# The first expert of a mixture-of-experts kernel: where its weight splitting, its last gate and its counts are issued

## The chip, the cores and the metric

The kernel runs on one core of a Trainium2 chip. The metric is the time of one execution in device microseconds, the median of several runs. The engines are named as the profile names them: PE (TensorE; PEld is its weight loading), DVE (VectorE), ACT (ScalarE), POOL (GpSimd), and SP (SyncE), which issues most of the DMAs. A "q" behind a name (PEldq, ACTq) is that engine's own sequencer.

## The reference, cut to what matters

```
def reference(...):                      # all in float32
    o = attention(q_l, k_l, v_l, q_g, k_g, v_g)      # 4 batches, 8 heads, 512 local + 32 global rows, 64 wide
    x = o as [2304, 512]                             # one token per row
    # mixture of 8 experts, one expert per token
    logits = x @ w_gate;  e_idx = argmax(logits)
    gate_w = softmax(logits)[e_idx];  eom = sigmoid(x @ w_output_gate)
    out[mask_e] = gate_w * eom[:, e] * (relu(x[mask_e] @ w1[e]) @ w2[e])      # w1 512x1024, w2 1024x512
    # a last layer
    h = out @ w_in;  g = P(h) / Q(h);  return g @ w_out
```

The routing depends on the data: how many tokens each expert has, and which, is known on the chip only when the gate of the last of four batches has run.

## The kernel before, in words

**Order of the program.** The order of the instructions is written out by hand. Python generators stand for streams of work, and a loop around the matrix products takes a step of such a stream at fixed places. Each engine executes its own instructions in the order in which the program issues them, so an instruction that waits holds up everything behind it on its engine.

**Precision.** Every factor is split into a high part (a cast on ACT, L696 for weights) and a low part (the difference, L700), and each product is three matmuls. `split_piece` makes one of 16 pieces (128x512) of an expert's weights; its mode says who makes the low part: "act" means DVE, "act_pool" means POOL. `split_set` goes through the pieces, and after every second one it issues the load of the next raw weights on SP's queue (L686), into the buffer that the two pieces have left.

**The first expert.** `wide(0, ...)` computes it for 296 tokens, taken from the first three batches, while the gate of the last batch still runs. It has 8 steps of a first product (L903, 12 matmuls) and 8 of a second (L915, 12 matmuls), the second two steps behind. After every six matmuls it takes one step of the stream `woven`. I call such a place a hook; there are 32.

- `woven` before: in hooks 1 to 16 two steps of the last gate (GS = 2), and from hook 9 on one piece of the first half of expert 1's weights, its low parts on POOL and DVE in turn. At hook 17 all that is left of the gate is issued at once, and with hook 17 the list PLAN0 begins: s is a piece of the second half (hooks 18 to 25), g a gather of token rows (two at hook 17), x a scaling of a gathered block on ACT (hooks 23, 24, 26, 27), p its transposition and splitting (`prep`, hooks 24, 25, 28, 30). `lists` (the list of tokens, transposed on PE at L650) runs at hooks 17 to 20.
- The gate's last batch: transposes on PE (L519), some small DVE instructions, the counting matmuls (L554), then five pairs of one-hot rows on DVE (L605, L609) that five matmuls (L620) turn into the table of tokens. From it come the row indices for the gathers (`places`). `counts` then makes the counts and offsets of the experts in 19 small DVE instructions (L747 to L767).
- After the 32 hooks `end` copies the result from PSUM (L921) and stores it. Then every engine loads the counts into registers, in two loads (L1058, L1060), and two branches follow: `single` for the third block of 128 tokens of expert 0 (L1064; it is taken in this run, L870 to L886), and a loop for the rest (L1066; skipped). Then the blocks 2 and 3 of expert 1 are scaled on ACT (L797), transposed on PE (L810) and split, and expert 1 begins (L903 with the tile xa).

The transposes of `prep` go through one PSUM tile (pt) as long as the first expert runs: the next block is transposed only when ACT (L790) and DVE (L791) have read the one before.

The weights of expert 0 itself are split during the attention before it (SM0 is the mode), the last pieces at its very end.

Of the kernel before, what the change touches and what calls it, by code (L numbers as in the profile page):

```python
# [11 lines left out]
I32 = mybir.dt.int32  # L12
# [7 lines left out]
B, H, SL, SG, D = 4, 8, 512, 32, 64  # L20
S = SL + SG
NT = B * S
NP = H // 2
DM = H * D
E = 8
F1 = 1024
NBLK = NT // 128
NCOL = E * NBLK


WN = 15
SLAST, GW, GS, SPL, AH = 1, 3, 2, 8, (0, 0, 14, 1, 2, 0, 2, 24, 2)
NW = 0
XR = lambda nc: nc.scalar.copy
XG = lambda nc, h: nc.vector.tensor_copy
# [6 lines left out]
BASE, MOST, FIRST, LAG = 256, 512, 296, 2  # L42
# [4 lines left out]
def plan(n, **at):  # L47

    o = [""] * n
    for t in "scxpg":  # L50
        for k in at.get(t, ()):
            o[k] += t
    return o
# [8 lines left out]
R7 = 4  # L62
L9 = {-1: (0, 1, 2, 3)}
XLO = lambda nc, i: (nc.vector, nc.gpsimd)[i % 2]
PLAN0 = plan(16, s=range(1, 9), g=(0, 0, 1, 2, 11, 12, 14, 15), x=(6, 7, 9, 10), p=(7, 8, 11, 13))
TR = (1, 1), (2, 2)
YC = 256
EL, EW = 0, 11
# [19 lines left out]
CH = (4, 3, 4, 3, 3)  # L88
ER = {"ab": 1, "q": 2, "u": 2, "r0": 1}
CQ = lambda nc: nc.sync  # L90
SM0 = "act_pool"
MASK = (0, 1, 2, 3, 1, 2, 3, 4)
KT, KV, KX = 4, 5, 7
KG, LL = 3, 2
# [9 lines left out]
class Build:  # L104
# [391 lines left out]
    def gate(self, b, xT=None, woven=0):  # L496
# [107 lines left out]
        for i in range(nb):  # L604
# [6 lines left out]
            for _ in range(2 + (OY if b < B - 2 else 0)):  # L611
                if i:
                    next(tail, None)
                yield
        for _ in wait():
            yield
        for _ in tail:
            yield
# [6 lines left out]
        if last:  # L625
            self.places(self.idx[:, 0:NCOL], self.tab)
            nc.gpsimd.memset(self.idx[:, NCOL:], NT)
            self.counts()
        elif b == B - 2:
            self.places(self.idx0, self.tab[:, 0:3])  # L630
            nc.vector.tensor_copy(self.cnt0, self.run_cnt[0:1, 0:1])
# [113 lines left out]
    def counts(self):  # L745
        nc, c = self.nc, self.cnt_f
        nc.vector.memset(c, 0.0)  # L747
        nc.vector.tensor_tensor(out=self.cnt_i[:, 0], in0=self.run_cnt[0:1, :], in1=self.small[0:1, 8:16], op=ALU.subtract)
        nc.vector.tensor_copy(c[:, 0, 1:8], self.cnt_i[:, 0, 0:7])
        for n, k in enumerate((1, 2, 4)):  # L750
            o = c[:, n + 1] if n < 2 else self.cnt_i[:, 1]
            nc.vector.tensor_copy(o[:, 0:k], c[:, n, 0:k])
            nc.vector.tensor_tensor(out=o[:, k:8], in0=c[:, n, k:8], in1=c[:, n, 0:8 - k], op=ALU.add)

        k, n0, o = self.cnt0, self.cnt_i[:, 0, 0:1], self.cnt_x
# [3 lines left out]
        nc.vector.scalar_tensor_tensor(out=o[:, 3:4], in0=n0, scalar=FIRST + 128, in1=o[:, 3:4], op0=ALU.is_gt, op1=ALU.max)  # L759
        nc.vector.tensor_scalar(out=o[:, 2:3], in0=n0, scalar1=127, scalar2=None, op0=ALU.add)  # L760
        nc.vector.tensor_scalar(out=o[:, 2:3], in0=o[:, 2:3], scalar1=7, scalar2=None, op0=ALU.logical_shift_right)
        nc.vector.tensor_tensor(out=o[:, 2:3], in0=o[:, 2:3], in1=o[:, 3:4], op=ALU.mult)

        f = o[:, 4:5]
        nc.vector.tensor_reduce(out=f, in_=self.cnt_i[:, 0], axis=AX.X, op=ALU.max)
        nc.vector.tensor_scalar(out=f, in0=f, scalar1=MOST, scalar2=None, op0=ALU.is_gt)
        nc.vector.scalar_tensor_tensor(out=f, in0=self.cnt_i[:, 1, E - 1:E], scalar=128 * CH[0], in1=f, op0=ALU.is_lt, op1=ALU.max)  # L767


    def expert_tiles(self, pool):  # L770
# [7 lines left out]
        self.cnt_i = cp.tile([1, 2, E], I32, name="cnt_i")  # L778
        self.cnt_f = cp.tile([1, 4, E], F32, name="cnt_f")
        c = cp.tile([1, 6], I32, name="cnt_x")  # L780
        self.cnt0, self.cnt_x = c[:, 0:1], c[:, 1:6]

    def gather(self, j, ix, n=NT, rows=128):

# [30 lines left out]
    def experts(self, st, first, gate):  # L815
# [114 lines left out]
                pass  # L930
            return end

        def todo(e, plan, half=None, blocks=(), gathers=()):


            sp = self.split_set(e + 1, SPLIT_MODE if e < E - 1 else MODE7, half)
            if e == E - 1:
                self.rest = sp
            k = NCONV * (e - 1)
            gs, xs, ps = iter(gathers), iter(blocks), iter(blocks)  # L940
            for do in plan:
                for c in do:
                    if c == "s":
                        next(sp, None)
                    elif c == "c":
                        self.conv_step(k)
                        k += 1
                    elif c == "g":
                        for eb in islice(gs, 1):
                            self.gather(eb[1], col(*eb))  # L950
# [79 lines left out]

        def woven():

            g, sp = self.gate(B - 1, woven=GW), todo(0, "s" * 8, 0)
            for n in count():
                for _ in range(GS):
                    next(g, None)
                if n >= SPL:
                    next(sp, None)
                yield
                if n >= WN:  # L1040
                    break
            for _ in g:
                pass
            for _ in sp:
                pass

            yield from weave(todo(0, PLAN0, 1, blocks(1, (0, 1)) + blocks(0, (2, 3)),
                                  blocks(1, (0, 1)) + blocks(0, (2, 3)) + blocks(2, (0, 1)) + blocks(1, (2, 3))),
                             self.lists())


        acc = [ps_a.tile([128, 512], F32, tag=f"acc{m}", name=f"acc{m}") for m in range(4)]
        wide(0, 0, FIRST, self.xs, woven(), False, acc)()
        gate.close()
        pools.append(PP("ps_t2", 1))
        self.conv_init(P("cv"))
        self.f32.append(spare)
        vals = nc.values_load_multi_w_load_instructions(self.cnt_i.rearrange("a b e -> a (b e)"), min_val=0, max_val=NT)[1]  # L1058
        cnt, off[:] = vals[:E], vals[E:]
        x = nc.values_load_multi_w_load_instructions(self.cnt_x, min_val=0, max_val=NBLK)[1]  # L1060
        more0, j0, end0, again0, rare = x
# [347 lines left out]
```

## Time and profile before

| | us |
|---|---|
| median of 3 runs (lowest, highest) | 834.62 (830.66, 835.91) |
| the profiled execution | 836.12 |
| its span in the trace | 834.6 |
| first expert: first L903 to first matmul of the third block (L870) | 152.98 to 194.89 |
| third block: to the first L903 of expert 1 | 194.89 to 214.02 |

PE is busy for 787.6 us of the span (94%), DVE 605.9, ACT 543.7, POOL 374.2. The mean granted clock of PE is 0.979 of full speed.

Two views are used most. The view by windows gives, for each stretch, the busy time of each engine and the clock that PE was granted (1.00 is 2.4 GHz, 0.50 is 1.2 GHz). The timeline merges equal instructions that follow each other into one row: start, duration, engine, line, operation, tiles and count, and in brackets how long the engine had been idle before and what it then waited for. The rows themselves stand below.

### The profile page before, as it was taken

Reading aid. Unit: us, or ns where it says so; the run is one execution under the profiler, and the core shown is the slowest. Engines: PE = TensorE matmul, PEld = TensorE weight load, DVE = VectorE, ACT = ScalarE, POOL = GpSimd, SP = SyncE. Lnnn points to the kernel's source line nnn. Section 1 sums busy time; section 2 is a strip of 40 time slices with the busy share of each in tenths; the row PEclk is TensorE's granted clock in tenths of the full one; section 3 lists DMA queues with packets and bytes.
Section 4 is the critical chain, followed back from the end, with each engine's and each line's share of the span. In section 5 each row is a group of like instructions: output and inputs, shape, how many; then the busy total and the mean of one; then the engine's idle time right before and its main releaser. Section 6 shows DMA issues by size and latency. Waiting matters only on the chain. (4 is left out here: it accounts for less than half of the span.)

```text
span 834.6 us, 17062 instructions
## 1 busy us (share of the span) xinstructions
PE 787.6 (94%) x6093; PEld 669.2 (80%) x6094; DVE 605.9 (73%) x1436; ACT 543.7 (65%) x1221; POOL 374.2 (45%) x422
## 2 busy tenths in 40 slices
PE   7999998969899999999998999999999999999995
PEld 4776766767898999998885788899878888988983
DVE  3769778681556777874377999778878885888784
ACT  3667776542645666663447888768777775788774
POOL 2445555561434665652253787532243234222432
PEclk7999999979899999999999999999999999999998
DMA  8899993464373988986263432010010001000100
GB/s 298 267 281 302 289 304 83 131 195 136 127 253 127 308 302 282 323 292 206 81 187 103 126 93 60 13 51 26 13 38 25 2 1 51 0 1 1 39 1 38
DMA packets 50957, 113.90 MB, mean 136 GB/s; under 512 B 8963, under 2 KB 22548, under 8 KB 48810
## 3 DMA queue, kind: packets, MB, share of 16 engines
q1 hardware_dynamic: 42202, 98.23, 36.6%
q0 software_dynamic: 4288, 10.06, 3.7%
q10 hardware_dynamic: 4368, 4.34, 1.5%
q8 instruction: 55, 0.90, 0.5%
q14 instruction: 44, 0.36, 0.1%
HBM read 96.99 MB, written 19.56 MB: 140 GB/s over the span
## 5 line engine op out<-in xcount | busy, mean ns | idle before, releaser
L1190 POOL TENSOR_TENSOR q<-q,ab 128x384 f32<-128x384 f32 (+1 forms) x80 | 101.8, 1273 | 203.2 <-ACT q L1189 195.0
L1226 PE MATMUL acc<-slot,gh 128*128 128x512 f32 x544 | 171.1, 395 | 3.8 <-ACT gh L1198 2.0
L700 POOL TENSOR_TENSOR slot<-raw,slot 128x512 fp32r<-128x512 f32 x80 | 111.1, 1393 | 78.9 <-ACT slot L696 74.4
L1119 PE MATMUL ph<-x2c,slot 128*128 128x512 f32 (+1 forms) x576 | 132.5, 379 | 5.7 <-DVE u L1192 3.9
L1119 PEld LDWEIGHTS ph<-x2c,slot 128*128 128x128 f32 x576 | 106.5, 189 | 26.3 <-DVE u L1192 5.1
L1226 PEld LDWEIGHTS acc<-slot,gh 128*128 128x128 f32 x544 | 101.1, 187 | 25.9 <-ACT gh L1198 2.9
L1226 PE MATMUL acc<-slot,gl 128*128 128x512 f32 x272 | 107.6, 396 | 0.2 <-DVE gl L1199 0.2
L915 PE MATMUL acc<-hT,slot 128*128 128x256 f32 (+1 forms) x768 | 105.2, 288 | 0.2 <-DVE hT L909 0.2
L915 PEld LDWEIGHTS acc<-hT,slot 128*128 128x128 f32 x768 | 98.0, 191 | 0.5 <-DVE hT L909 0.4
L696 ACT CAST slot<-raw 128x512 fp32r<-128x512 f32 x144 | 85.0, 618 | 9.0 <-DVE yt L921 5.9
L1201 ACT ACTIVATE r<-q,cab 128x384 f32<-128x384 f32 (+1 forms) x80 | 52.8, 660 | 46.1 <-POOL q L1190 45.9
L1207 DVE SCALAR_TENSOR_TENSOR q<-q,r 128x384 f32<-128x384 f32 (+1 forms) x64 | 38.0, 593 | 52.2 <-ACT r L1203 52.1
L316 POOL TENSOR_SCALAR pr<-ex,r 128x128 f32<-128x128 f32 x128 | 47.0, 380 | 60.6 <-PE sc L263 16.9
L1119 PE MATMUL ph<-xa,slot 128*128 128x384 f32 x384 | 72.0, 336 | 1.5 <-DVE u L1214 1.5
L1198 ACT CAST gh<-u 128x384 fp32r<-128x384 f32 (+1 forms) x80 | 44.6, 557 | 41.7 <-DVE u L1214 34.8
L1119 PEld LDWEIGHTS ph<-xa,slot 128*128 128x128 f32 x384 | 67.7, 188 | 4.6 <-DVE u L1214 1.9
L700 DVE TENSOR_TENSOR slot<-raw,slot 128x512 fp32r<-128x512 f32 x64 | 61.1, 958 | 13.3 <-ACT slot L696 12.3
L1226 PEld LDWEIGHTS acc<-slot,gl 128*128 128x128 f32 x272 | 50.9, 187 | 13.4 <-DVE gl L1199 1.0
L298 ACT ACTIVATE ex<-sm,mx 128x128 f32<-128x128 f32 x128 | 50.3, 395 | 16.1 <-POOL pr L316 8.0
L1189 ACT ACTIVATE q<-ab,cab 128x384 f32<-128x384 f32 (+1 forms) x80 | 59.8, 747 | 0.0
L1188 ACT ACTIVATE u<-ph,cab 128x384 f32<-128x384 f32 (+1 forms) x80 | 56.8, 710 | 0.0
L1192 DVE SCALAR_TENSOR_TENSOR u<-u,cab,ph 128x384 f32<-128x384 f32 (+1 forms) x80 | 53.4, 668 | 2.8
(215 smaller groups left out, 1510.3 us busy)
## 6 DMA issues: line engine op xcount, KB each, us to landing
raw<-in_w_dram SPq DMA_DIRECT2D x76, 512.0 KB
vw<-in_vw_dram SPq DMA_DIRECT2D x16, 1024.0 KB
r<-in_w_dram SPq DMA_DIRECT2D x20, 512.0 KB
kw<-in_kw_dram SPq DMA_DIRECT2D x16, 384.0 KB
raw<-wf SPq DMA_DIRECT2D x10, 512.0 KB
xg<-ybuf SPq DMA_DIRECT2D x17, 256.0 KB
qt<-in_qT_dram SPq DMA_DIRECT2D x32, 128.0 KB
xbuf<-xrow SPq DMA_DIRECT2D x8, 512.0 KB
```

The source lines that it names most:

```text
L298: nc.scalar.activation(ex[:, h], src[:, h], AF.Exp, bias=mx[:, h:h + 1], scale=-1.0, accum_out=ssum[:, h:h + 1])
L316: nc.gpsimd.tensor_scalar(out=pr[:, h], in0=ex[:, h], scalar1=r[:, h:h + 1], scalar2=1.0, op0=ALU.mult, op1=ALU.mult)
L696: nc.scalar.copy(hi, r)
L700: eng.tensor_tensor(out=lo[:, c], in0=r[:, c], in1=hi[:, c].bitcast(F32), op=ALU.subtract)
L915: nc.tensor.matmul(acc[m][:, :n], lhsT=W[:, b, 8 + f, 128 * m:128 * m + 128], rhs=hT[f % nh][:, a, :n], start=(f == 0 and i == 0), stop=(f ...
L1119: self.nc.tensor.matmul(ph[:, :w], lhsT=l[a], rhs=r[b], start=(k == 0 and i == 0), stop=(k == 3 and i == 2))
L1188: nc.scalar.activation(u, h, AF.Identity, scale=a3, bias=a2)
L1189: nc.scalar.activation(q, ab, AF.Identity, scale=b1, bias=b0)
L1190: nc.gpsimd.tensor_tensor(out=q, in0=q, in1=ab, op=ALU.mult)
L1192: nc.vector.scalar_tensor_tensor(out=u, in0=u, scalar=a1, in1=h, op0=ALU.add, op1=ALU.mult)
L1201: nc.scalar.activation(r0, q, AF.Ln, bias=eps1)
L1226: nc.tensor.matmul(accs[i], lhsT=l[a], rhs=Wo[:, b, f, :], start=(f == 0 and j == 0), stop=(f == 15 and j == 2))
```

## The change

The change moves work of the first expert to other hooks and other engines:

- The last three pieces of expert 0's weights, and the first half of expert 1's (8 pieces), get their low parts on DVE; the second half (8 pieces) gets them all on POOL.
- The gate takes three steps per hook (GS = 3), and waits 11 steps, not 3, between the last one-hot rows and the matmuls on them (TAW). Its steps then end in hook 17.
- The first half's pieces are issued at hooks 7, 10, 13, 16 and 18, 20, 21, 22 (PLANA), the second half's at hooks 24 to 31. With the gathers at hooks 18, 18, 19, 20, 30, 31, 32, 32, the scalings at 24, 25, 27, 28 and the preps at 26, 27, 30, 32 they make PLANB, which begins at hook 18, as do `lists` (18 to 21).
- `counts` is cut into seven steps at hooks 21 to 27 (PLANC).
- The counts lie in one tile and are loaded into registers once. The loads stand ahead of `end`.
- The blocks 2 and 3 of expert 1 are scaled on POOL, ahead of the branch to the third block. The skipped branch gathers and scales block 3 again.

```diff
-WN = 15
-SLAST, GW, GS, SPL, AH = 1, 3, 2, 8, (0, 0, 14, 1, 2, 0, 2, 24, 2)
+SLAST, GW, GS, TAW, AH = 1, 3, 3, 11, (0, 0, 14, 1, 2, 0, 2, 24, 2)
...
-PLAN0 = plan(16, s=range(1, 9), g=(0, 0, 1, 2, 11, 12, 14, 15), x=(6, 7, 9, 10), p=(7, 8, 11, 13))
+PLANA = plan(26, s=(6, 9, 12, 15, 17, 19, 20, 21))
+PLANB = plan(18, s=range(6, 14), g=(0, 0, 1, 2, 12, 13, 14, 14), x=(6, 7, 9, 10), p=(8, 9, 12, 14))
+PLANC = plan(12, k=(3, 4, 5, 6, 7, 8, 9))
...
-SM0 = "act_pool"
+SM0 = ("act_pool",) * 13 + ("act",) * 3
...
-        for _ in wait():
+        for _ in range(TAW) if last else wait():
             yield
         for _ in tail:
             yield
...
             nc.gpsimd.memset(self.idx[:, NCOL:], NT)
-            self.counts()
...
+        c = self.cnts = cp.tile([1, 2 * E + 6], I32, name="cnts")
+        self.cnt_i, self.cnt_x, self.cnt0 = c[:, 0:2 * E].rearrange("a (b e) -> a b e", b=2), c[:, 2 * E:-1], c[:, -1:]
...
-            g, sp = self.gate(B - 1, woven=GW), todo(0, "s" * 8, 0)
-            for n in count():
-                for _ in range(GS):
-                    next(g, None)
-                if n >= SPL:
-                    next(sp, None)
+            g, sp, end = self.gate(B - 1, woven=GW), todo(0, PLANA, 0, mode="act"), object()
+            while True:
+                more_ = [next(g, end) for _ in range(GS)]
+                next(sp, None)
                 yield
-                if n >= WN:
+                if end in more_:
                     break
...
-            yield from weave(todo(0, PLAN0, 1, blocks(1, (0, 1)) + blocks(0, (2, 3)),
-                                  blocks(1, (0, 1)) + blocks(0, (2, 3)) + blocks(2, (0, 1)) + blocks(1, (2, 3))),
-                             self.lists())
+            yield from weave(sp, todo(0, PLANB, 1, blocks(1, (0, 1)) + blocks(0, (2, 3)),
+                                      blocks(1, (0, 1)) + blocks(0, (2, 3)) + blocks(2, (0, 1)) + blocks(1, (2, 3)), mode="act_pool"),
+                             self.lists(), todo(0, PLANC))
...
-        wide(0, 0, FIRST, self.xs, woven(), False, acc)()
+        stored = wide(0, 0, FIRST, self.xs, woven(), False, acc)
...
+        vals = nc.values_load_multi_w_load_instructions(self.cnts[:, 0:-1], min_val=0, max_val=NT)[1]
+        cnt, off[:] = vals[:E], vals[E:2 * E]
+        more0, j0, end0, again0, rare = vals[2 * E:]
+        j0, end0 = (nc.s_assert_within(x, 0, NBLK) for x in (j0, end0))
+        stored()
...
+        for b in (2, 3):
+            self.scale(b, 128, "p")
         with tc.If(more0 > 0):
             single(0, 2, self.xs, put=store_rest)
         with tc.If(again0 > 0):
             fetch(0, j0)
             more(0, j0, end0)
+            self.gather(3, col(1, 3))
+            self.scale(3, 128, "p")
         for b in (2, 3):
-            self.scale(b, 128, S1)
             self.prep(b, self.xa, ps_t(), 128 * b, scale=False)
```

## Rows read from the trace of the kernel before

**Rows 1.** Windows of two us; PE, PEld, DVE, ACT, POOL busy, PE clock, DMA.

```profile
172.00:174.00 2.00, 1.08 (x5) 0.72 (x3) 1.75 (x16) 1.17 (x3) 0.43 (x1) 0.50 0.76 170
212.00:214.00 2.00, 0.74 (x4) 0.74 (x5) 0.69 (x1) 1.21 (x2) 0.00 (x0) 0.62 0.33 131
```

**Rows 2.** Timeline of PE in the first expert.

```profile
162.40 1.81 PE L915 MATMUL acc<-hT,slot 128*128 128x296 f32 x12
164.06 1.79 PE L903 MATMUL ph<-xs,slot 128*128 128x296 f32 x12
...
171.47 1.61 PE L915 MATMUL acc<-hT,slot 128*128 128x296 f32 x6
174.48 0.47 PE L650 MATMUL lgT<-ident,wrap 128*128 128x128 f32 x1 [1.40 <-DVE wrap L646]
174.60 1.83 PE L915 MATMUL acc<-hT,slot 128*128 128x296 f32 x6
176.23 2.75 PE L903 MATMUL ph<-xs,slot 128*128 128x296 f32 x12
...
185.35 1.11 PE L810 MATMUL pt<-ident,xg 128*128 128x128 f32 x4 [3.19 <-DVE xa L791]
186.12 1.83 PE L903 MATMUL ph<-xs,slot 128*128 128x296 f32 x6
187.74 2.20 PE L915 MATMUL acc<-hT,slot 128*128 128x296 f32 x12
```

**Rows 3.** Groups, shapes apart, 153 to 194.3 us: busy, mean ns, idle before.

```profile
L785 POOL DMA_INDIRECT xg<-xbuf,idx x8 | 9.0, 1128 | 11.6 <-DVE cnt_x L760 5.1 <-ACT xs L790 2.9 <-ACT xa L790 1.6
...
L620 PE MATMUL ta<-ob,oa 128*128 128x136 f16 x5 | 0.9, 223 | 1.7 <-DVE ob L609 1.7
```

**Rows 4.** Timeline of DVE in the first expert.

```profile
154.55 0.42 DVE L523 TENSOR_REDUCE L<-lg 128x64 f32<-128x256 f32 x1 [3.60 <-PE lg L519]
...
163.82 1.30 DVE L605 TENSOR_SCALAR oa<-iota,slf 128x128 f16<-128x128 f16 x1
...
168.70 0.21 DVE L605 TENSOR_SCALAR oa<-iota,slf 128x128 f16<-128x128 f16 x1
...
174.07 0.15 DVE L767 SCALAR_TENSOR_TENSOR cnt_x<-cnt_i,cnt_x 1x1 int32<-1x1 int32 x1
...
180.04 4.66 DVE L700 TENSOR_TENSOR slot<-raw,slot 128x512 fp32r<-128x512 f32 x1
```

**Rows 5.** Timeline of POOL in the same time.

```profile
163.70 2.62 POOL L700 TENSOR_TENSOR slot<-raw,slot 128x512 fp32r<-128x512 f32 x2 [2.19 <-ACT slot L696]
...
180.41 3.73 POOL L700 TENSOR_TENSOR slot<-raw,slot 128x512 fp32r<-128x512 f32 x3
```

**Rows 6.** Tile raw, 140 to 216 us: duration ns min/median/max, starts.

```profile
L696 ACT CAST slot<-raw x21: 608/618/632, 146.7 to 214.9; 128x512 fp32r<-128x512 f32 x21
L700 POOL TENSOR_TENSOR slot<-raw,slot x14: 1262/1288/1456, 140.9 to 215.6; 128x512 fp32r<-128x512 f32 x14
...
L700 DVE TENSOR_TENSOR slot<-raw,slot x8: 670/684/4657, 162.3 to 185.2; 128x512 fp32r<-128x512 f32 x8
```

**Rows 7.** Timeline of PE around the third block.

```profile
194.89 4.43 PE L870 MATMUL ph<-slot,xs 128*128 128x512 f32 x18 [0.67 <-ACT yt L921]
200.15 0.66 PE L857 MATMUL pt<-ident,hr 128*128 128x128 f32 x4 [0.83 <-ACT hr L873]
...
213.26 1.11 PE L810 MATMUL pt<-ident,xg 128*128 128x128 f32 x4 [1.30 <-ACT xg L797]
```

**Rows 8.** Line L1060, the second register load of PE: ns, start.

```profile
L1060 PEldq TENSOR_LOAD <-cnt_x x1: 1251/1251/1251, 193.4 to 193.4; - x1
```

**Rows 9.** Line L1066, the skipped branch, on POOL's sequencer.

```profile
L1066 POOLq INC_SWDGE_SEM x1: 437/437/437, 211.6 to 211.6; - x1
```

**Rows 10.** POOL's scaling of 544 columns in the attention: ns, starts.

```profile
L320 POOL TENSOR_SCALAR exg<-exg,r x8: 712/725/738, 18.5 to 129.3; 128x544 f32<-128x544 f32 x8
```

**Rows 11.** Waits of SP's queue, 186 to 216 us: total, times, longest.

```profile
SPq L686 <- DVE slot L700: 22.9, 1, 22.9
```

More of the change, by code (lines that the diff above doesn't have):

```diff
@@ L49, in plan @@
     o = [""] * n
-    for t in "scxpg":
+    for t in "scxpgk":
         for k in at.get(t, ()):
@@ L749, in counts @@
         nc.vector.tensor_copy(c[:, 0, 1:8], self.cnt_i[:, 0, 0:7])
+        yield
         for n, k in enumerate((1, 2, 4)):
@@ L753, in counts @@
             nc.vector.tensor_tensor(out=o[:, k:8], in0=c[:, n, k:8], in1=c[:, n, 0:8 - k], op=ALU.add)
+            yield
         k, n0, o = self.cnt0, self.cnt_i[:, 0, 0:1], self.cnt_x
@@ L759, in counts @@
         nc.vector.scalar_tensor_tensor(out=o[:, 3:4], in0=n0, scalar=FIRST + 128, in1=o[:, 3:4], op0=ALU.is_gt, op1=ALU.max)
+        yield
         nc.vector.tensor_scalar(out=o[:, 2:3], in0=n0, scalar1=127, scalar2=None, op0=ALU.add)
@@ L762, in counts @@
         nc.vector.tensor_tensor(out=o[:, 2:3], in0=o[:, 2:3], in1=o[:, 3:4], op=ALU.mult)
+        yield
         f = o[:, 4:5]
@@ L767, in counts @@
         nc.vector.scalar_tensor_tensor(out=f, in0=self.cnt_i[:, 1, E - 1:E], scalar=128 * CH[0], in1=f, op0=ALU.is_lt, op1=ALU.max)
+        yield
     def expert_tiles(self, pool):
@@ L931, in wide, with todo @@
             return end
-        def todo(e, plan, half=None, blocks=(), gathers=()):
-            sp = self.split_set(e + 1, SPLIT_MODE if e < E - 1 else MODE7, half)
+        def todo(e, plan, half=None, blocks=(), gathers=(), mode=SPLIT_MODE):
+            sp = self.split_set(e + 1, mode if e < E - 1 else MODE7, half)
             if e == E - 1:
@@ L939, in todo @@
             k = NCONV * (e - 1)
-            gs, xs, ps = iter(gathers), iter(blocks), iter(blocks)
+            gs, xs, ps, ns = iter(gathers), iter(blocks), iter(blocks), self.counts()
             for do in plan:
@@ L947, in todo @@
                         k += 1
+                    elif c == "k":
+                        next(ns, None)
                     elif c == "g":
@@ L1031, in woven @@
         def woven():
-            g, sp = self.gate(B - 1, woven=GW), todo(0, "s" * 8, 0)
-            for n in count():
-                for _ in range(GS):
-                    next(g, None)
-                if n >= SPL:
-                    next(sp, None)
+            g, sp, end = self.gate(B - 1, woven=GW), todo(0, PLANA, 0, mode="act"), object()
+            while True:
+                more_ = [next(g, end) for _ in range(GS)]
+                next(sp, None)
                 yield
-                if n >= WN:
+                if end in more_:
                     break
[L1042 to L1045, printed above, removed]
-            yield from weave(todo(0, PLAN0, 1, blocks(1, (0, 1)) + blocks(0, (2, 3)),
-                                  blocks(1, (0, 1)) + blocks(0, (2, 3)) + blocks(2, (0, 1)) + blocks(1, (2, 3))),
-                             self.lists())
+            yield from weave(sp, todo(0, PLANB, 1, blocks(1, (0, 1)) + blocks(0, (2, 3)),
+                                      blocks(1, (0, 1)) + blocks(0, (2, 3)) + blocks(2, (0, 1)) + blocks(1, (2, 3)), mode="act_pool"),
+                             self.lists(), todo(0, PLANC))
         acc = [ps_a.tile([128, 512], F32, tag=f"acc{m}", name=f"acc{m}") for m in range(4)]
-        wide(0, 0, FIRST, self.xs, woven(), False, acc)()
+        stored = wide(0, 0, FIRST, self.xs, woven(), False, acc)
         gate.close()
@@ L1057, in experts @@
         self.f32.append(spare)
[L1058 to L1061, printed above, removed]
+        vals = nc.values_load_multi_w_load_instructions(self.cnts[:, 0:-1], min_val=0, max_val=NT)[1]
[3 more added lines that the diff above has]
+        stored()
         self.off = off
         self.conv_first()
+        for b in (2, 3):
+            self.scale(b, 128, "p")
         with tc.If(more0 > 0):
```

3 lines of the change are left out of this document (removed).

## The prediction

> **What bounds the kernel now.** I read the windows first, to find where PE stands still; then PE's timeline there, for what it waits for; then DVE and POOL beneath, for why that is late. PE is the bound of the first expert: 32 hooks of six matmuls. At full clock twelve matmuls follow the last twelve after 1.66 us (starts 162.40 and 164.06), so six take 0.83; a row of twelve lasts 1.80, 0.14 more than its stretch, a row of six thus 0.97 [rows 2]. 32 hooks are 26.6 us, with the small matmuls and transposes some 30; the table ahead shows 41.9. The reader is to see two holes. At the first PE waits 1.7 us in all for the one-hot rows [rows 3], then 1.40 for `wrap`, and works at half the clock [rows 1, 2]. At the second it waits 3.19 us for the low part of a gathered block and falls to slow rows again [rows 2]. Both have DVE behind them: a one-hot row of 0.21 us takes 1.30 while POOL makes low parts (two from 163.70 to 166.32), and a low part of DVE, 0.68 at the median, takes 4.66 from 180.04, until POOL's three, begun at 180.41, are through at 184.14 [rows 4 to 6].
>
> **The sum, part by part** (us; minus is gained).
>
> (a) The gate without POOL's low parts, its five matmuls later. Nothing of POOL's reads beside DVE until the gathers of hook 18, and between the last one-hot rows (hook 10) and the matmuls (hook 14) lie over three hooks. The 1.7 goes [rows 3]: -1.7, at worst 0. New: two low parts of expert 0 stand on DVE ahead of the gate's first reduction, 2 x 0.68 [rows 6], and the counting matmuls come at hook 4 instead of 6. No row shows what PE would wait there: between 0 and these 1.4. DVE had been idle for 3.60 before that reduction [rows 4], which most of them fill, so I take a value near none: +0.3.
>
> (b) `wrap` behind the counts. The last of 19 count instructions starts at 174.07, `wrap` follows, PE had waited 1.40 [rows 2, 4]. The counts now come three hooks later; late next is one low part of 0.68 in front of `wrap`, against 1.66 until its transpose: -1.4, at worst -0.7.
>
> (c) The clock behind the first hole. Three rows at half clock against full: (1.61 - 0.97) + (1.83 - 0.97) + (2.75 - 1.80) = 2.45 [rows 2]; the clock there is 0.50, the lower level of 1.2 GHz, after PE had stood still [rows 1]. Without the hole: -2.4, at worst 0.
>
> (d) The second hole. In hooks 24 to 32 DVE has no low parts of weights any more; what it does there reads PSUM, apart from the counts. Late next are two things. ACT is crowded: eight casts of 0.62 [rows 6], four scalings and four preps now lie in nine hooks of 0.83, where the casts began six hooks earlier before. And count instructions stand on DVE ahead of the first prep's low part, on which the second prep's transposes wait. I leave 1.5 of the 3.19: between nothing and the 4.66 of the row just cited, nearer to one wait of 1.30: -1.7, ends -3.2 and +1.5.
>
> (e) The clock behind it: (1.11 - 0.66) + (1.83 - 0.97) + (2.20 - 1.81) = 1.7, the 0.66 from the same transposes at full clock [rows 2, 7]. Standstills of 0.67 and 0.83 have transposes of full speed behind them [rows 7]; 1.5 lies nearer to these than to 3.19: -1.7, at worst 0.
>
> (f) Into the third block. Before, 0.67 [rows 7], under the second register load of 1.25 [rows 8]. One load goes, but the last prep now stands behind the last matmul (hook 32, not 30), so nothing covers the load that follows it: 1.25 idle for 0.67, +0.6, ends -0.7 and +1.3.
>
> (g) PE waits 0.83 for ACT's `hr` [rows 7], because ACT reads its registers between the copies and that instruction. The loads now stand ahead of the copies: -0.8, at worst 0. The copies and the store of the block come later; nothing in the third block's first products reads them.
>
> (h) The scalings on POOL. Before, the transposes of block 3 waited 1.30 for ACT, until 213.26 [rows 7]. POOL is behind by then: from hook 24, 8 x 1.29 and four gathers of 1.13 [rows 3, 6] are 14.8 in nine hooks of some 9.5 with the preps, so 5 late; with a load like 1.25, a landing of a gather, and 2 x 0.73 [rows 10] it ends some 11 into the 19 of the third block. That is hidden; were the cover gone, `prep` and then expert 1 would wait. Late next is POOL's skipping of the loop: the skipped part now also writes block 3, so its transposes wait until POOL has passed, 211.6 + 0.44 = 212.0 [rows 9]. With a hop of 0.3: -0.9, ends 0 and -1.3. The clock falls here too, to 0.62 over the window [rows 1]; since PE still stands still I take no gain of it.
>
> Costed at nothing: the third low part of expert 0 on DVE (0.68, in the same 3.60 of idle time); the raw loads on SP, from hooks 10, 12, 14, 16, 19, 21, 23, 25 to 10, 16, 20, 22, 25, 27, 29, 31. A piece of hook 30 reads what hook 22 loads, eight hooks or 6.6 us later, and after the last SP has 22.9 us to wait for the next free buffer [rows 11]; without this the casts would wait, and PE with them. The stores of the gate's factors on SP now come before hook 10's load, not behind several. The early gathers stand as near to the table as before.
>
> The sum: -1.7 + 0.3 - 1.4 - 2.4 - 1.7 - 1.7 + 0.6 - 0.8 - 0.9 = **-9.7**. Against the profiled execution 836.12 - 9.7 = 826.4; the median lies 1.5 below that execution, so 834.62 - 9.7 = **824.9**. What follows runs at PE's pace or shifts as a whole, so I let the gain stand to the end.
>
> **The rivals.**
>
> 1. The counts run into POOL's low parts. Four two-input instructions of the counts (L753, L757, L759, L762) stand on DVE before the low part at hook 26, while POOL makes eight low parts on end. If each waits for one of 1.29, that is 5.2: the second hole and its clock stay, (d) turns from -1.7 to +2.0 at worst and (e) to 0. 824.9 + 3.4 = 828.3 with the hole as it was, 830.3 at worst. For it: the one-hot row of 1.30. Against it: ACT feeds POOL at about POOL's pace, which leaves gaps, and some of the counts can run before POOL begins. The Trainium skill, "SBUF — State Buffer", "Who interferes with whom", speaks against the change here: a DVE instruction with two SBUF inputs and a GpSimd instruction that reads SBUF exclude each other for the whole of the first. By that rule every such count can lose a whole low part; the 1.30 agrees, while the 4.66 passed three of POOL's. Chance 0.29.
>
> 2. Slower: DVE is kept out for POOL's whole run, as at 180.04 for three [rows 4, 5], and from hook 18 on, where gathers begin. Then `wrap` is late again ((b), (c) to 0: +3.8), and the low part at hook 26 waits for some 11 of POOL's 14.8: (d) +7.8 instead of -1.7, (e) 0. 824.9 + 3.8 + 9.5 + 1.7 = 839.9. It is slower than before as soon as PE stands 8 us or more at hook 27 and the first hole stays. Against it: ACT's pace. Chance 0.06, half of it over 1%.
>
> 3. The holes only move: with three gate steps per hook DVE falls behind and PE waits at hooks 4 and 14 about what it waited before; (a), (b), (c) gone, the rest kept: 824.9 + 5.2 = 830. The one-hot rows are 0.21 where POOL makes no low part [rows 4], which is against it. Chance 0.08, with all ways in which hardly anything changes.
>
> 4. More: (d) in full, and PE's clock stays up into expert 1 at the price of (e): 824.9 - 1.5 - 1.7 = 821.7. Chance 0.14.
>
> **The numbers.** Forecast 0.43, with a range of its own from 822.5 to 828. Measurement of this kernel tells a change from none from about 1%, here 826.3. Below it lie rival 4 (0.14), most of the forecast (0.34) and a little of rival 1: faster 0.50. Same: the rest of the forecast, rival 1, rival 3 and half of rival 2: 0.46. Slower: 0.04. The range takes in rivals 4, 1 and 3: **819 to 832**.
>
> **What would show it.** In the changed kernel's profile: one-hot rows near 0.21 and no wait at L620; no wait at L650; the clock at 1.00 throughout the first expert; DVE's L791 beside POOL's L700 at its usual length, and PE's wait for the second prep below 2; the first L870 near 187; `hr` without a wait. The prediction is wrong if count instructions of a us and more stand beside POOL's low parts (rival 1), or if PE waits for ACT's scalings or for POOL at the end of the third block.

## The result and the profile after

| us | before | after |
|---|---|---|
| median (lowest, highest), runs in turn on one chip | 832.71 (830.66, 835.91) | 822.13 (820.92, 824.43) |
| the profiled execution | 836.12 | 824.43 |
| its span | 834.6 | 822.9 |
| ahead of the first expert | 152.98 | 153.98 |
| first expert, to the first matmul of the third block | 41.91 | 32.69 |
| third block, to the first matmul of expert 1 | 19.13 | 16.99 |
| from there to the end | 620.6 | 619.2 |

The ratio is 0.9873 with a 95% interval of [0.9828, 0.9918], clear of 1: faster, by 10.6 us (1.3%) where 9.7 were forecast. Between the two profiled executions lie 11.7: +1.0 - 9.2 - 2.1 - 1.4, in the order of the last four rows. The first term I don't put down to the change: it lies ahead of the first expert, and over the profiles of the experiments below that have the changed kernel's code there this part runs from 150.56 (e10) to 154.44 us (e12). The last is a part that I had given no price.

Lines have moved by 1 to 4: L907 is the old L903, L919 L915, L621 L620, L814 L810, L874 L870, L861 L857, L794 and L795 are L790 and L791, L801 L797, L759 L757, L1068 L1066.

The timeline of PE in the changed kernel answers to [rows 2, 7]:

```profile
153.98 1.08 PE L907 MATMUL ph<-xs,slot 128*128 128x296 f32 x6 [0.49 <-ACT lgs L464]
...
157.95 0.28 PE L555 MATMUL pr<-ohb,tri 128*128 128x40 bf16 x5
...
167.38 0.35 PE L621 MATMUL ta<-ob,oa 128*128 128x136 f16 x3
...
171.83 0.27 PE L650 MATMUL lgT<-ident,wrap 128*128 128x128 f32 x1
...
176.85 0.60 PE L814 MATMUL pt<-ident,xg 128*128 128x128 f32 x4
177.21 1.06 PE L919 MATMUL acc<-hT,slot 128*128 128x296 f32 x6
179.95 0.66 PE L814 MATMUL pt<-ident,xg 128*128 128x128 f32 x4 [1.68 <-DVE cnts L763]
180.36 2.71 PE L919 MATMUL acc<-hT,slot 128*128 128x296 f32 x18
...
186.67 4.44 PE L874 MATMUL ph<-slot,xs 128*128 128x512 f32 x18 [1.17 <-ACT xs L794]
190.95 0.60 PE L861 MATMUL pt<-ident,hr 128*128 128x128 f32 x4
...
200.98 0.63 PE L814 MATMUL pt<-ident,xg 128*128 128x128 f32 x4 [0.59 <-PEq L1068]
202.93 1.08 PE L814 MATMUL pt<-ident,xg 128*128 128x128 f32 x4 [1.32 <-DMA xg<-xbuf,idx]
203.66 5.62 PE L907 MATMUL ph<-xa,slot 128*128 128x256 f32 x36
```

No row of the gate has a wait (brackets) any more, nor has `wrap` at L650. One hole is left, 1.68 us before the second preparation, and the 18 matmuls behind it take 2.71, the length of full speed. In the groups the five matmuls on one-hot rows have 0.0 idle, against 1.7 [rows 3]:

```profile
L621 PE MATMUL ta<-ob,oa 128*128 128x136 f16 x5 | 0.8, 229 | 0.0
```

The windows of the changed kernel (columns as in [rows 1]): the clock is at 1.00 where it was 0.50 before, and falls once, at the start of expert 1.

```profile
172.00:174.00 2.00, 2.00 (x17) 2.00 (x17) 1.74 (x8) 0.95 (x3) 1.70 (x2) 1.00 0.77 189
...
202.00:204.00 2.00, 1.07 (x5) 1.10 (x6) 0.69 (x1) 0.23 (x1) 0.23 (x1) 0.66 0.37 137
204.00:206.00 2.00, 2.00 (x12) 2.00 (x11) 0.69 (x1) 1.72 (x3) 0.76 (x1) 0.50 0.00 0
206.00:208.00 2.00, 2.00 (x18) 2.00 (x18) 1.05 (x3) 1.56 (x4) 1.59 (x2) 0.98 0.00 0
```

What stands under the hole of 1.68? First DVE, which PE waits for at the end; then POOL; then ACT, all in the changed kernel:

```profile
175.24 3.18 DVE L759 SCALAR_TENSOR_TENSOR cnts<-cnts 1x1 int32<-1x1 int32 x1
...
178.51 0.15 DVE L761 SCALAR_TENSOR_TENSOR cnts<-cnts 1x1 int32<-1x1 int32 x1
179.20 0.69 DVE L795 TENSOR_TENSOR xa<-pt,xa 128x512 fp32r<-128x512 f32 x1 [0.54 <-ACT xa L794]
```

```profile
171.76 1.24 POOL L789 DMA_INDIRECT xg<-xbuf,idx  x1 [0.30 <-issue]
...
174.83 1.01 POOL L789 DMA_INDIRECT xg<-xbuf,idx  x1 [0.30 <-issue]
175.86 2.53 POOL L700 TENSOR_TENSOR slot<-raw,slot 128x512 fp32r<-128x512 f32 x2
```

```profile
175.50 0.60 ACT L696 CAST slot<-raw 128x512 fp32r<-128x512 f32 x1
177.46 0.72 ACT L801 ACTIVATE xg<-xg 128x512 f32<-128x512 f32 x1 [1.35 <-DMA xg<-xbuf,idx]
178.09 0.60 ACT L696 CAST slot<-raw 128x512 fp32r<-128x512 f32 x1
178.59 0.57 ACT L794 CAST xa<-pt 128x512 fp32r<-128x512 f32 x1
```

A count of one element is held for 3.18 us on DVE, from a gather on POOL through two of POOL's low parts: what rival 1 described. Yet it ends at 178.42, two more counts are through at 178.66, and DVE then idles 0.54 for ACT's cast. ACT is what is late: it stood 1.35 in order before a scaling whose gather (issued at 171.76) had not landed, while the transposed block had been ready since 177.5. The counts come next, and not far behind: had ACT been in time, they would have held DVE's low part until 178.66, so that PE would still have waited about 1.1 (my estimate, 1.68 - 0.54). The release that the PE row names (`cnts`) is the instruction of DVE behind the one that matters.

### The profile page after: what moved, and what is told of

It reads as the page before. It is cut to its first block, busy times and chain, and to the rows that moved or that the text cites. A ratio compares the mean times of both kernels' runs of the same rounds, so it can differ in the third digit from the quotient of the medians.

```text
span 822.9 us, 17044 instructions
## 1 busy us (share of the span) xinstructions
PE 781.7 (95%) x6093; PEld 664.5 (81%) x6094; DVE 603.5 (73%) x1439; ACT 542.2 (66%) x1219; POOL 370.2 (45%) x421
## 5 line engine op out<-in xcount | busy, mean ns | idle before, releaser
L700 POOL TENSOR_TENSOR slot<-raw,slot 128x512 fp32r<-128x512 f32 x77 | 106.9, 1392 | 69.8 <-ACT slot L696 68.2
L919 PE MATMUL acc<-hT,slot 128*128 128x256 f32 (+1 forms) x768 | 103.5, 285 | 0.3 <-DVE hT L913 0.3
L919 PEld LDWEIGHTS acc<-hT,slot 128*128 128x128 f32 x768 | 96.2, 189 | 0.5 <-DVE hT L913 0.5
L700 DVE TENSOR_TENSOR slot<-raw,slot 128x512 fp32r<-128x512 f32 x67 | 59.2, 888 | 15.2 <-ACT slot L696 14.1
```

The lines of the kernel that those rows point to most:

```text
L700: eng.tensor_tensor(out=lo[:, c], in0=r[:, c], in1=hi[:, c].bitcast(F32), op=ALU.subtract)
L919: nc.tensor.matmul(acc[m][:, :n], lhsT=W[:, b, 8 + f, 128 * m:128 * m + 128], rhs=hT[f % nh][:, a, :n], start=(f == 0 and i == 0), stop=(f ...
```

## The experiments

Each edit is against the changed kernel, unless said otherwise. "Stretch" is the first expert from its first matmul to the first of the third block (32.69 in the changed kernel), "block" the third block to expert 1 (16.99).

| run | median (lowest, highest), us | ratio to before | stretch, block |
|---|---|---|---|
| e1 engines alone | 828.25 (825.89, 830.67) | 0.9951 [0.9926, 0.9977] | 34.64, 19.63 |
| e2 all but the engines | 828.07 (826.20, 830.82) | 0.9950 [0.9922, 0.9977] | 37.04, 16.95 |
| e3 counts back | 821.90 (820.39, 823.39) | 0.9874 [0.9825, 0.9924] | 32.73, 16.56 |
| e4 scalings back | 825.44 (824.01, 829.72) | 0.9929 [0.9894, 0.9963] | 32.76, 18.05 |
| e5 loads back | 824.26 (819.82, 824.96) | 0.9868 [0.9804, 0.9931] | 32.94, 16.83 |
| e6 counts early | 821.93 (820.15, 824.35) | 0.9856 [0.9797, 0.9916] | 32.40, 16.62 |
| e7 preps first | 821.81 (819.67, 825.55) | 0.9866 [0.9806, 0.9926] | 32.83, 15.84 |
| e8 e6 and e7 | 820.93 (819.13, 822.31) | 0.9846 [0.9788, 0.9903] | 32.89, 15.82 |
| e9 changed kernel again | 821.44 (819.88, 827.64) | 0.9902 [0.9865, 0.9938] | 32.60, 16.54 |
| e10 e8 again | 820.37 (819.25, 821.82) | 0.9875 [0.9843, 0.9906] | 33.08, 15.84 |
| e11 short pause | 823.25 (819.79, 826.21) | 0.9904 [0.9870, 0.9937] | 34.03, 16.88 |
| e12 e8, later prep | 820.20 (819.25, 822.88) | 0.9847 [0.9814, 0.9880] | 33.12, 15.83 |

e1 to e4 ran on one chip (before 832.57), e5 to e8 on another (834.81), e9 to e11 on a third (831.59), e12 on a fourth (833.45).

**e1: the kernel before, with the engines of the low parts alone.**

```diff
-SM0 = "act_pool"
+SM0 = ("act_pool",) * 13 + ("act",) * 3
...
-            g, sp = self.gate(B - 1, woven=GW), todo(0, "s" * 8, 0)
+            g, sp = self.gate(B - 1, woven=GW), todo(0, "s" * 8, 0, mode="act")
...
-  ... blocks(2, (0, 1)) + blocks(1, (2, 3))),
+  ... blocks(2, (0, 1)) + blocks(1, (2, 3)), mode="act_pool"),
```

> The kernel before with only the engines of the low parts changed (expert 0's last three and expert 1's first half on DVE, the second half on POOL); hooks, gate, counts, loads and scalings as before. Theory A (both holes of the first expert are DVE held up by POOL's low parts): one-hot rows near 0.21, no wait at the five matmuls (1.7 before), the 3.19 of the second hole down to about 1; the 1.40 for wrap stays, since the 19 counts still stand ahead of it. First L903 to first L870 is 35 to 37 us, not 41.9; the time 826 to 828 beside 832.7. Rival B (the gain comes from the new pacing of gate and counts): 40 to 42 us for the stretch, within 2 us of the kernel before.

The wait for one-hot rows is gone and the second hole is 0.85, but the wait for `wrap` grows to 2.63, where I had expected the 1.40 of before. On DVE the 19 counts stand ahead of it, from 169.12 to 171.42. The clock stays at 1.00 behind this wait. The stretch is a little under the 35 to 37 expected, the time a little over the 826 to 828. PE's timeline in e1, and the window behind the wait:

```profile
171.75 0.33 PE L650 MATMUL lgT<-ident,wrap 128*128 128x128 f32 x1 [2.63 <-DVE wrap L646]
...
178.57 0.66 PE L810 MATMUL pt<-ident,xg 128*128 128x128 f32 x4 [0.85 <-DVE xa L791]
...
192.37 0.65 PE L857 MATMUL pt<-ident,hr 128*128 128x128 f32 x4 [1.33 <-ACT hr L873]
```

```profile
172.00:174.00 2.00, 2.00 (x17) 2.00 (x16) 0.07 (x1) 1.31 (x3) 1.74 (x2) 1.00 0.64 195
```

**e2: the change without the engines.** The reverse: `SM0` and both `mode=` arguments as before.

> The changed kernel with the engines of the low parts as before (POOL and DVE in turn in both halves, all of expert 0's on POOL); the new hooks, counts, loads and scalings stay. Theory A: POOL's low parts stand in the gate again and DVE's beside POOL's eight hooks before the end, so the stretch (first L907 to first L874) grows from 32.7 us to 37 to 40 and the time to 826 to 829. Rival B: 33 to 35 us, 822 to 824.

Here the rest of the change meets POOL's low parts. PE's timeline, its windows, and DVE and POOL at the first wait:

```profile
157.23 0.28 PE L555 MATMUL pr<-ohb,tri 128*128 128x40 bf16 x5 [1.83 <-DVE ohb L546]
...
180.28 1.11 PE L814 MATMUL pt<-ident,xg 128*128 128x128 f32 x4 [2.73 <-DVE cnts L763]
```

```profile
180.00:182.00 2.00, 1.72 (x8) 1.72 (x9) 1.55 (x6) 0.56 (x2) 0.00 (x0) 0.50 0.54 203
```

```profile
153.32 2.15 DVE L527 COPY L<-Lg 128x16 f32<-128x16 f32 x1
```

```profile
151.96 2.54 POOL L700 TENSOR_TENSOR slot<-raw,slot 128x512 fp32r<-128x512 f32 x2 [1.07 <-ACT slot L696]
154.44 1.00 POOL L827 MEMSET xg<- 128x513 f32 x2
```

A copy of 16 columns takes 2.15, from 153.32 to 155.47: past the end of POOL's two low parts (154.50), to that of its two memsets (155.44). PE waits 1.83 for the counting matmuls at hook 4. Theory A held (37.04, 828.07). PE has no wait for the one-hot rows, in e2 as in e1: to be rid of it the engines were enough, and so were the later matmuls (here with PE held up by 1.83 ahead of them).

Either part alone is worth 4.3 (e1) or 4.5 (e2), both 10.6. e1 keeps a wait for `wrap` and the third block of before (19.63). e2 has the new wait of 1.83 and 2.73 of the second hole, with the clock at 0.50 behind it.

**e3: all counts at the end of the gate, as before.** (`self.counts()` run through where the change took it out; PLANC dropped.)

> The changed kernel with the 19 counts issued at once at the end of the gate (hook 17), as before. They take 2.4 us on DVE ahead of wrap, which has 1.7 us until its transpose: PE waits 0.5 to 1.5 at L650. In return no count stands beside POOL's low parts, so the 3.18 of one count and PE's 1.68 at the second prep shrink to about 0.5. Theory A: about even, 822 give or take 1.5. Rival B (the pacing of the counts carries gain): 2 to 3 us slower than the changed kernel, and the clock falls behind L650.

Theory A held. PE waits 0.87 for `wrap` and 0.59 at the second preparation; the stretch is the same 32.7, and the median lies within the changed kernel's runs. The counts' new place is worth nothing by itself. PE in e3 (L652 and L816 are L650 and L814 here):

```profile
171.48 0.33 PE L652 MATMUL lgT<-ident,wrap 128*128 128x128 f32 x1 [0.87 <-DVE wrap L648]
...
178.58 0.66 PE L816 MATMUL pt<-ident,xg 128*128 128x128 f32 x4 [0.59 <-DVE xa L797]
```

The two waits hang together. The second gather is issued as early as in the changed kernel (17.80 us into the stretch, there 17.78), but behind its wait for `wrap` PE comes to the first preparation 1.1 later, and ACT to its first scaling 0.9 later. So ACT has no landing to wait for.

**e4: the scalings back on ACT, behind the branches.**

```diff
-        for b in (2, 3):
-            self.scale(b, 128, "p")
         with tc.If(more0 > 0):
...
-            self.gather(3, col(1, 3))
-            self.scale(3, 128, "p")
         for b in (2, 3):
+            self.scale(b, 128, S1)
```

> The changed kernel with blocks 2 and 3 of expert 1 scaled on ACT behind the two branches, as before. By the prediction's term (h): first L874 to the first L907 of expert 1 grows from 17.0 us to about 18 (0.9 more; up to 1.3). Rival: the skipped branch sets that time in both (PE waited for POOL's passing of it in the changed kernel), and the stretch stays at 17.0 within 0.3.

The block is 1.06 longer, and the waits before the two transposes, 1.60 and 1.29, are those of before (1.30 for the second [rows 7]). The first in the kernel before, then both in e4:

```profile
211.31 0.65 PE L810 MATMUL pt<-ident,xg 128*128 128x128 f32 x4 [1.60 <-ACT xg L797]
```

```profile
201.20 0.66 PE L814 MATMUL pt<-ident,xg 128*128 128x128 f32 x4 [1.60 <-ACT xg L801]
203.15 1.11 PE L814 MATMUL pt<-ident,xg 128*128 128x128 f32 x4 [1.29 <-ACT xg L801]
```

The median moved by more than that: on the same chip e3, whose counts change nothing in the time, has 821.90, 3.5 less. Between these two profiles e4's block is 1.5 longer, and what follows the block 2.2. Of the 2.2, 1.08 lie in expert 1's first 36 matmuls (5.64 against 4.56), where the clock fell in e4 and stayed up in e3 (below); the rest was not looked into.

**e5: two register loads, behind `end`, as before**; the counts stay in one tile.

```diff
-        stored = wide(0, 0, FIRST, self.xs, woven(), False, acc)
+        wide(0, 0, FIRST, self.xs, woven(), False, acc)()
...
-        vals = nc.values_load_multi_w_load_instructions(self.cnts[:, 0:-1], ...)[1]
+        vals = nc.values_load_multi_w_load_instructions(self.cnts[:, 0:2 * E], ...)[1]
+        x = nc.values_load_multi_w_load_instructions(self.cnts[:, 2 * E:-1], ...)[1]
...
-        stored()
```

> The changed kernel with the copies and stores of the first expert ahead of the register loads again, in two loads. By the prediction's term (g): PE waits 0.8 to 1.3 us for hr in the third block, which the changed kernel does not; by (f) PE's standing still before the block, 1.17, grows by no more than the second load, to between 1.2 and 2.0. The stretch from the first L907 to the first L907 of expert 1 is 0.8 to 2 us longer than the changed kernel's 49.7. Rival (loads hidden anyway): within 0.4.

The rival came: the stretch and the block make 49.77, beside 49.68. PE starts the third block after 1.38 instead of 1.17, and there is still no wait for `hr`. ACT's loads tell why. Before:

```profile
L1058 ACTq TENSOR_LOAD <-cnt_i x1: 2021/2021/2021, 195.3 to 195.3; - x1
...
L1060 ACTq TENSOR_LOAD <-cnt_x x1: 1967/1967/1967, 197.4 to 197.4; - x1
```

And in e5:

```profile
L1057 ACTq TENSOR_LOAD <-cnts x1: 2435/2435/2435, 187.5 to 187.5; - x1
...
L1059 ACTq TENSOR_LOAD <-cnts x1: 563/563/563, 190.0 to 190.0; - x1
```

Before, ACT was done at 199.4 and made `hr` at 199.50; in e5 the second load takes 0.56, not 1.97, and ACT is ready at 190.6, before PE needs it. That the one tile is what shortens the second load was not tried by itself; in e1, with two tiles, ACT's second load took 1.14 behind a first of 3.35, and PE waited 1.33 for `hr`.

**e6: the counts spread more to the front.**

```diff
-PLANC = plan(12, k=(3, 4, 5, 6, 7, 8, 9))
+PLANC = plan(12, k=(2, 2, 3, 3, 4, 4, 5))
```

> The changed kernel with the seven steps of the counts at hooks 20, 20, 21, 21, 22, 22, 23, ahead of POOL's low parts, not 21 to 27. If the count instruction of 3.18 us is DVE waiting for POOL's two low parts, no count takes over 0.3 now, and PE's 1.68 at the second prep falls to the 0.6 that the kernel with the counts at the gate's end showed, with no wait at L650: 1 us less than the changed kernel in the stretch. Rival (ACT's crowding and a late gather, for which ACT waited 1.35, set that wait): it stays at 1.3 to 1.7.

Neither side came out clean. The last count is still held, for 2.47 where I had expected 0.3 at most. The hole is 1.26, between the 0.6 of the theory and the 1.3 to 1.7 of the rival, and ACT's wait for the gather 0.95. As in the changed kernel DVE is through with the counts before ACT's cast, and then idles for it, 0.57 (there 0.54). DVE in e6:

```profile
174.35 2.47 DVE L771 SCALAR_TENSOR_TENSOR cnts<-cnts 1x1 int32<-1x1 int32 x1
177.40 0.69 DVE L795 TENSOR_TENSOR xa<-pt,xa 128x512 fp32r<-128x512 f32 x1 [0.57 <-ACT xa L794]
```

**e7: the preparations ahead of the skipped branch.** It leaves out the second gather, which is needed where that branch is taken; here it is skipped.

```diff
+        for b in (2, 3):
+            self.prep(b, self.xa, ps_t(), 128 * b, scale=False)
         with tc.If(again0 > 0):
             fetch(0, j0)
             more(0, j0, end0)
-            self.gather(3, col(1, 3))
-            self.scale(3, 128, "p")
-        for b in (2, 3):
-            self.prep(b, self.xa, ps_t(), 128 * b, scale=False)
```

> The changed kernel with the preps of expert 1's blocks 2 and 3 ahead of the second branch (the loop that is skipped) and no second gather of block 3 in that branch. Theory: what PE waits for at the end of the third block, 0.59 and 1.32 before the two preps, is not the scaling (done some 3 us earlier) but POOL's passing of the skipped branch. Then both preps follow the third block at once, and expert 1 waits only for ACT's passing of the branch behind them, some 0.7: first L874 to expert 1's first L907 falls from 17.0 to about 16, and the clock has less reason to fall. Rival: the waits are for the scalings and stay.

Both waits of 0.59 and 1.32 are gone, and 0.72 for the branch stays. The block is 15.84, 1.15 shorter than in the changed kernel's first profile, where the clock fell at its end, and 0.70 shorter than in e9's, where it stayed up. PE in e7:

```profile
197.22 1.39 PE L814 MATMUL pt<-ident,xg 128*128 128x128 f32 x8
199.33 4.58 PE L907 MATMUL ph<-xa,slot 128*128 128x256 f32 x36 [0.72 <-ACTq L1070]
```

**e8: e6 and e7 together; e9: the changed kernel again; e10: e8 again, beside e9.**

> Both of the last two edits together. If they are independent: 2 us less than the changed kernel by the waits, 820 beside 822, and one to two more where the clock stays up at expert 1's start. Rival: what is saved at the first shows again as a wait for POOL at the second, and it is no faster than the better of the two alone.

> The changed kernel once more, with nothing altered, so that the next two kernels stand against it on the same chip. Expected: 822 +- 1.5 us, ratio to the kernel before about 0.987. If it comes out above 826 or below 819, the differences of 1 us among the kernels run so far are those of chips and not of kernels.

> The changed kernel with the counts spread more to the front (2, 2, 3, 3, 4, 4, 5 a step), the first block of expert 1 prepared ahead of the skipped branch, and no second gather for it. Theory: the two waits of 0.59 and 1.32 us ahead of expert 1 go, a new one of 0.72 stays, so about 1.2 us less, and the clock at expert 1's first matmuls stays at full level: 1 to 2 us below the changed kernel on the same chip (820 to 821 beside 822). Rival: the wait is only moved, the two agree within 0.5 us.

e9 came out as expected. On one chip 820.37 (e10) stands beside 821.44 (e9). That is about what the block gives (0.70 between their profiles), but the intervals of the two ratios overlap: e8 is the lowest kernel by median in both sessions, not one shown to be faster than the change. Nothing shows that the early counts add to it: e8's stretch is 32.89, e7's 32.83.

**e11: the pause ahead of the one-hot matmuls cut to 3** (`TAW` 11 to 3), all that follows three hooks earlier.

> The changed kernel with the pause between the counts and the one-hot matmuls cut from 11 steps of the first expert to 3 less eight, so that the gathers of the second half are issued some three steps earlier. Theory: the last one-hot rows are done on VectorE about 2 us after TensorE would reach that place, so TensorE waits 1 to 2 us at L621, and gains a part back since the gathers land earlier (the wait ahead of the second preparation falls from 1.68 to below 1): 0 to 1.5 us slower than the changed kernel. Rival: no wait at L621, and the whole is 1 us faster.

PE did not wait at L621: the rival was right there, and the pause of 11 is longer than needed. But no time was gained: the second preparation waited 2.19, and the clock fell behind it (0.50 over 178 to 180), so the stretch is 1.4 longer than in e9. PE in e11:

```profile
176.46 0.66 PE L814 MATMUL pt<-ident,xg 128*128 128x128 f32 x4 [2.19 <-DVE cnts L763]
...
183.47 2.71 PE L919 MATMUL acc<-hT,slot 128*128 128x296 f32 x18
186.02 4.36 PE L874 MATMUL ph<-slot,xs 128*128 128x512 f32 x18
```

Here ACT waited 1.50 for the first gather and then worked off its order: from 172.01 on a scaling, two casts, a scaling, an activation and a cast, and the preparation's cast at 175.10, for a block transposed by 173.5. My reason for the wait (DVE's rows) fell, and its place too. The last rows show one thing more: with the last preparation three hooks earlier PE goes into the third block without a wait.

**e12: e8 with the second preparation one hook later** (`p=(8, 9, 12, 14)` to `(8, 10, 12, 14)`).

> The changed kernel with the counts spread to the front, the first block of expert 1 prepared ahead of the skipped branch (both as in the pair run before), and in addition the second preparation one hook later (at hook 28, not 27). Theory: what PE waits for at the second preparation is ACT, whose casts of the first one stand in order behind a scaling that waits for a gather to land; two hooks of other matmuls lie between the two preparations instead of one, so the wait of 1.68 (2.06 in the pair run before) falls to about 0.4, the stretch from the first L907 to the first L874 from 32.7 to about 31.3, and the median by about 1.3 below that pair (820.4), to 819 to 820. Rival: ACT is behind by its sum of work and not by one landing; then the wait comes back at the third preparation and the stretch stays within 0.4 of 32.7.

The rival came: 1.11 at the second preparation and 0.75 at the third make 1.86, beside 2.06 in e10, and the stretch did not move (33.12 and 33.08). ACT waited 1.69 for the landing and then worked without a break from 178.19 to the third preparation's cast at 182.38, for a block transposed by 181.3. So both are in it: one landing makes ACT late, and the work that stands in order behind it leaves no room to catch up. PE in e12:

```profile
180.68 0.66 PE L814 MATMUL pt<-ident,xg 128*128 128x128 f32 x4 [1.11 <-DVE xa L795]
...
183.74 0.66 PE L814 MATMUL pt<-ident,xg 128*128 128x128 f32 x4 [0.75 <-DVE xa L795]
```

**The hole and ACT's wait, over the runs.** ACT's longest wait for the landing in this place, and PE's wait behind it:

| | e3 | e6 | after | e5 | e9 | e8 | e7 | e4 | e10 |
|---|---|---|---|---|---|---|---|---|---|
| ACT for the gather | 0 | 0.95 | 1.35 | 1.43 | 1.45 | 1.47 | 1.52 | 1.62 | 1.94 |
| PE for the preparation | 0.59 | 1.26 | 1.68 | 1.71 | 1.57 | 1.79 | 1.82 | 1.74 | 2.06 |

They rise together, if not in strict order. Not in the table are e1 and e2, where DVE or POOL has other low parts in this place (e2: 1.30 and 2.73), and e11 and e12, with preparations at other hooks. e3's 0.59 is the chain alone: transpose, cast, low part, next transpose. e6, e8 and e10 are the same up to this place, so the landing itself varies by a us. That ACT loses this time and can't make it up by the third preparation is what e12 shows; that a faster gather would close the hole wasn't tried, and by the estimate above the counts on DVE would still keep most of it open in the changed kernel.

**The clock at the start of expert 1.** Where the transposes before it waited 1.6 and 1.3 (before, e1, e4) the clock fell in all three profiles. With 0.6 and 1.2 to 1.3 it fell in three (after, e2, e11) and stayed in four (e3, e5, e6, e9). Without these waits (e7, e8, e10, e12) it stayed in all four. The change's own kernel shows both; in e9:

```profile
202.00:204.00 2.00, 2.00 (x19) 2.00 (x18) 1.06 (x2) 2.00 (x5) 1.20 (x1) 1.00 0.00 0
```

Its first 36 matmuls take 4.56 where the first profile's took 5.62.

## Why the prediction was right

The forecast case came by its gain: measured against the kernel before on the same chip it is 10.6 for 9.7. The time, 822.13 for 824.9, lies in the range of 819 to 832, but 0.4 below the 822.5 to 828 that the forecast case had of its own; 1.9 of the distance is that the median of before was 832.71 in that session, not 834.62. It stands nearer to rival 4 (821.7) than to 824.9, but of that rival only one half came, and only now and then: the second hole did not close (1.68 is left), but the clock stayed up into expert 1 in some executions.

Two of the signs by which the prediction was to be wrong showed too. A count of 3.18 us stood beside POOL's low parts, and PE waited 1.32 at the end of the third block until POOL had passed the skipped branch (through at 202.7, PE's transposes at 202.93). Neither undid its term. The count was hidden by a later ACT, which I had not foreseen; POOL's passing is what (h) itself names as late next, so that sign was badly put.

| term | predicted | measured | from |
|---|---|---|---|
| (a) one-hot rows | -1.7 + 0.3 | -1.7 | no wait at L621, none at L555 |
| (b) `wrap` | -1.4 | -1.4 | no wait at L650 |
| (c) clock behind it | -2.4 | -2.4 | clock 1.00, rows of full length |
| (d) second hole | -1.7 | -1.5 | 3.19 to 1.68 |
| (e) clock behind it | -1.7 | -1.7 | transposes 0.66, then 18 matmuls in 2.71 |
| (f) into the third block | +0.6 | +0.5 | 0.67 to 1.17 |
| (g) `hr` | -0.8 | -0.8 | no wait at L861 |
| (h) scalings on POOL | -0.9 | -1.1 | e4 |
| sum | -9.7 | -10.1 | |

The two stretches became 9.2 + 2.1 = 11.3 shorter. The rows thus leave 1.2 that no term holds; 1.0 of it is in the first expert. There my way of counting (idle time and the length of rows) misses what PE loses about a standstill. Half of it can be read off: before, the five matmuls on one-hot rows hold PE for 0.76 beside their waits (168.16 to 170.57, less 1.65 idle), after the change for 0.22. The rest stays open. That the sums come so close to the measured gain is in part luck: the terms make 10.1, the medians 10.6, the two profiles 11.7.

**Right with its reason.** (a): in e1, without POOL's low parts in the gate, the wait at the matmuls goes though they stand as early as before. In e2, with POOL's low parts, it goes too, with the matmuls later, but a DVE instruction of the gate's first steps is held for 2.15 instead. (b): e1 leaves the counts in front of `wrap`, and they make it 2.63 late; but e3 says that once the matmuls are paced, counts in front cost only 0.87, which the second hole gives back. (h): the waits for ACT went, what is late next is POOL's passing of the skipped branch, as said (e7 takes it out, with PE's own: 0.7 with the clock up). The clock in (e) followed its hole. In (c) it hung on the waits for one-hot rows more than on `wrap`: before, it fell between 171.50 and 171.75, ahead of that wait (the six matmuls from 171.47 already take 1.61 [rows 2]), and in e1, without the waits for one-hot rows, it stayed at 1.00 behind 2.63 for `wrap`. Why it did there is not shown.

**Right in size, off in its reason.** (d): ACT is late, one of the two causes named, but what makes it late is a landing, which the term doesn't name; its crowded order only keeps it late (e12). The counts, the other cause, come second by 0.54. The 1.5 left was a guess between two ends, and that 1.68 came is luck. (f): the load took 1.81 and not 1.25, and began at 184.6, under the last matmuls. That the place of the last preparation uncovers it was right: in e11, with that preparation three hooks earlier, a load of 1.81 begins at 183.5, is through under the matmuls, and PE has no wait. (g): the wait was ACT's register loads, but the place of the loads is not what ended it: e5 undoes the place and costs 0.2. What is left of the change there is the one tile for the counts, which was not tried alone.

**Rival 1** (0.29) came in its mechanism and not in its price: counts were held for 3.18 and 1.22 beside POOL. They end before ACT does, so DVE still waits for ACT. The Trainium skill, "SBUF — State Buffer", "Who interferes with whom", says that of a DVE instruction with two SBUF inputs and a GpSimd instruction that reads SBUF the later one blocks until the first is finished, and that a DVE copy can take the shared ports as well. The runs agree on the blocking, for the copy too (2.15 in e2). They differ on its length: the count of 3.18 passed two of POOL's low parts. The 1.30 that the prediction set beside the rule is not of its kind: a one-hot row has one tensor as input, and it was held for one low part where the count of 3.18 was held for two.

**What had no price.** The clock at expert 1's start: I took no gain, because PE still stands still there. The two profiles are 1.4 apart from there to the end, 1.26 of it in the first 36 matmuls (6.88 before, 5.62 after). The clock fell in both, for a shorter time after the change. The tally above shows the changed kernel with and without the fall, so a median of several runs gains a part of it.

## What to carry to other kernels

When one engine holds up another on the critical path, both take the work of the one out of that stretch and pace the work of the other: e1 and e2 show that either alone gives less than half (4.3 and 4.5 of 10.6). A stall of some us on an engine costs nothing as far as that engine would then wait for another; look at what its next instruction waits for before you price it. The release that a row names can be an instruction beside the one that matters: follow the chain one engine further.

## What was not expected of the hardware

- A one-element instruction on DVE beside GpSimd took 3.18 us, 3.27 in e10, against 0.14 to 0.15 alone. Both times it ended within 0.03 us of the end of GpSimd's two low parts. Not every instruction is held so long: before, two one-hot rows of 1.30 and 1.33 got in one behind each of two low parts on end (163.70 to 166.32).
- A register load took 1.2 to 3.4 us an engine, but 0.56 to 1.09 for a second one from the same tile right behind it (e5); from another tile it was 1.09 to 3.25 (before, e1).
- The length of a standstill doesn't tell by itself whether the clock falls: behind 2.63 us (e1) and 2.06 (e10) it stayed at 1.00, behind 2.19 (e11) it went to 0.50.
- One kernel's executions differ with the clock: the changed kernel's profiles have spans of 822.9 (mean clock 0.988) and 819.3 (0.991). Of these 3.6 us 1.8 lie ahead of the first expert, where the clock of 80 to 120 us is 0.96 in the one and 1.00 in the other.
